# Both inverse transforms of a spectral block: frequencies 256 to 291, real and imaginary, in one chunk of 128 rows

## The chip, the cores and the metric

The kernel runs on one core of one Trainium2 chip. The metric is the time of one launch in device microseconds (us), the median of several runs. Lower is better.

## The reference

One adaLN block with two branches, forward and backward in one launch. `x` is 2048 x 576. A conditioning vector `c` gives six rows (`sa, ca, ga, sb, cb, gb`) by `silu(c) @ w_mod`. Cut to what matters:

```python
h = _layernorm(x) * (1 + ca) + sa
X = jnp.fft.rfft2(h)                      # 2048 x 289, complex
y = jnp.fft.irfft2(X * (w_r + 1j * w_i), s=(2048, 576))
x = x + ga * y
h = _layernorm(x) * (1 + cb) + sb
x = x + gb * (((h @ w_gate) * (h @ w_up)) @ w_down)     # 576 -> 4608 -> 576
```

The outputs are this `x` and the gradients (the vector-Jacobian product with `grad_out`) of `A_x`, `w_r`, `w_i`, `w_gate`, `w_up`, `w_down`, `c` and `w_mod`. The backward pass holds a second spectral chain of the same form, with the conjugate filter. So there are two inverse transforms: one in the forward pass, giving `y`, and one in the backward pass, giving the gradient of `h`.

## The kernel before

Everything is in bf16 with float32 sums in PSUM. The 2048 rows lie as 16 tiles of 128 (`NT = 16`). A transform over rows and columns is made of matmuls with tables: `RD` (real transform of the 576 columns), `G1` and `BD2` (the 2048 rows, split into 128 x 16), and for the way back `BDA`, `GB` and `IR`.

The order of the program is this. Tile pools lie in SBUF as two stacks, left and right, and a tile that takes over bytes of an earlier one waits until that one has been read. A scheduler orders the instructions of each engine when the program is built. Each engine and each DMA-issuing queue (SP, POOL) then works strictly in that order.

1. Forward, first stage (0 to 64 us): norm, columns, rows of the first transform (`s1_*`, zp and vp).
2. Forward, chunk stage (64 to 131 us): 19 chunks of up to 16 frequencies (`NCH = 19`). `s2_turn`, `s2_filter`, `s2_back`, `s2_inv` go through each. `s2_inv` (L420) ends with the first half of the inverse transform along the rows, in PSUM (`ap_`), and ScalarE copies it to `A_h`: 128 x 2 (real, imaginary) x 16 tiles x 292 frequencies (`FP = 292`, of which 289 are real ones).
3. Forward inverse transform, third stage (131 to 206 us), one step per tile `sa`. `s3_rows` (L449) ends the transform along the rows for three groups of 128 frequencies, starting at 0, 128 and 164 (`FS`; the last overlaps the second, and `IR` is zero for rows counted twice). Each group needs two matmuls of 256 columns, `upa` for two groups, `upb` for the third. ScalarE copies `upa` to `ut`, VectorE copies `upb` (L459). `s3_cols` (L461) goes back to 576 columns: for each half of 288 columns, six matmuls (three groups by real and imaginary) into `yp` (L471), so 12 per tile. `s3_norm` adds the residual and normalizes; it loads `xc` (L481) and turns the result by a DMA transpose into `h2T` (L499).
4. As a filler in stages 2 and 3 and alone until 300 us: `u4_group` (L351), the product of `grad_out` with `w_down`. It loads `wdn` (L358), turns it by DMA transpose into `wdT` (L359), multiplies into `u4p` (L364), stages into two buffers `ghh_st`, and POOL's queue writes these to `ghhT_d` (L367).
5. The middle (300 to 1262 us): the gated product and its gradients: gup (L611), u8p (L640) and the weight gradients u57p (L558). Weight gradients are copied to `so`, turned by DMA transpose into `woT` (L569) and stored. `product` of index 0 reads `gon`, the scaled `grad_out`, which lies at the top of a long-lived pool, up to byte 77536 of each partition.
6. Backward, first stage (1262 to 1364 us): `t1_*`, with the last u57p as filler. SP loads `n2c`, `goc`, `yc` (L813) for two tiles at a time. csA, csB, csC (L747) are sums over rows for the gradient of `c`. `trp` (L844) turns `gyr`, a ring of three buffers.
7. Backward, chunk stage (1364 to 1428 us): `t2_*`, again 19 chunks. `t2_inv` (L955) fills `A_`, the backward counterpart of `A_h`. `filter_grad` makes the gradients of `w_r` and `w_i` from `Xn`, loaded by POOL. The filler is now u3p (L1091), the down projection: 16 tiles x 2 halves x 36 matmuls. It needs `hl` (L1077), and `w_down` as `wdA` (blocks 0 to 14) and `wdB` (15 to 35), loaded by SP (L1066).
8. Backward inverse transform (1428 to 1480 us): `t3_rows` (L980), `t3_cols` (L992, yp at L1000), `t3_norm` (L1004, with csD, csE, and ScalarE's and VectorE's jk, u, ob). Here ScalarE copies both parts of `ut` (L989, L990). `opca_h` is a row that `t3_norm` needs; SP loads it (L709).
9. The rest of u3p, the remaining `filter_grad`s and the gradients of `c` and `w_mod` (to 1610 us).

`RD` and `IR` share one slot of SBUF (tag `tA`), once in each pass, and so do `G1` and `GB` (`tB`). POOL loads `IR` and `GB` in the backward pass.

Of the kernel before, what the change touches and what calls it, by code (L numbers as in the profile page):

```python
# [9 lines left out]
FP32 = mybir.dt.float32  # L10
BF = mybir.dt.bfloat16
# [3 lines left out]
ACT = mybir.ActivationFunctionType  # L15
# [4 lines left out]
NT = 16  # L20
S = 2048
D = 576
DP = 640
DF = 289
FP = 292
# [10 lines left out]
def _tables():  # L36
    f8 = np.float64
    q = np.arange(128)
    RD = np.zeros((128, 5, 2, FP), f8)
    f = np.arange(DF)  # L40
    for m in range(5):
        d = 128 * m + q
        valid = d < D
        ang = 2 * np.pi * np.outer(d, f) / D
        RD[:, m, 0, :DF] = np.cos(ang) * valid[:, None]
        RD[:, m, 1, :DF] = -np.sin(ang) * valid[:, None]
    t = np.arange(16); k1 = np.arange(128)
# [17 lines left out]
    for fc in range(3):  # L65
        ff = FS[fc] + q
        valid = (ff < DF) & (ff >= 128 * fc)
        cf = np.where((ff == 0) | (ff == DF - 1), 1.0, 2.0) / (D * S) * valid
        ang = 2 * np.pi * np.outer(ff, d) / D
        IR[:, fc, 0, :] = np.cos(ang) * cf[:, None]  # L70
        IR[:, fc, 1, :] = -np.sin(ang) * cf[:, None]
# [8 lines left out]
TABS = dict(RD=[128, 5, 2, FP], G1=[128, NT, 3, 128], GB=[128, NT, 3, 128], BD2=[128, 128], BDA=[128, 128], IR=[128, 3, 2, D])  # L80


def build(ctx, tc, A_x, A_w_r, A_w_i, B_w_gate, B_w_up, B_w_down, c_in, w_mod, grad_out,
          out_0, out_1, out_2, out_3, out_4, out_5, out_6, out_7, out_8):
    nc = tc.nc
# [57 lines left out]
    def norm_stats(xt, pool, nt, name, rstd_out, room=None):  # L143
# [43 lines left out]
    with ExitStack() as hs:  # L187
# [185 lines left out]

        u4_groups(4)
        r1.close()
        A_h = pool("hA", 1).tile([128, 2, NT, FP], BF, name="A_h")
        with ExitStack() as rc:
            c2 = pool("hc2", 2, "right", stack=rc)
            hwm = pool("hwm", 2, "right", stack=rc)
# [40 lines left out]
            def s2_inv(ci):  # L420
                g0, ng, f0, w = dims(ci)
                ap_ = fps.tile([128, 4, 128], FP32, name="ap_", tag="fp")
                for j in range(ng):
                    nc.tensor.matmul(ap_[:, j, :], lhsT=YTs[ci][:, j, :], rhs=T["BDA"][:], start=True, stop=True)
                Ac = A_h[:].rearrange("k c a f -> k (c a) f")[:, :, f0:f0 + w].rearrange("k e (j f) -> k j e f", f=4)
                evac(Ac, ap_[:, 0:ng, :].rearrange("k j (e f) -> k j e f", f=4), eng="a")

            def s2_fill(ci):
                u4_groups(2)
# [17 lines left out]
        uts, ybs, h2_made = {}, {}, []  # L447

        def s3_rows(sa):  # L449
            ut = uts[sa] = hw2.tile([128, 3, 256], BF, name="ut", bufs=3)  # L450
            upa = fps.tile([128, 2, 256], FP32, name="upa", tag="fp")
            upb = fps.tile([128, 2, 256], FP32, name="upb", tag="fp")
            for fc in range(3):
                f0 = FS[fc]
                o = upa[:, fc, :] if fc < 2 else upb[:, 0, :]
                nc.tensor.matmul(o, lhsT=A_h[:, 0, sa, f0:f0 + 128], rhs=T["GB"][:, sa, 1:3, :].rearrange("k v s -> k (v s)"), start=True, stop=False)
                nc.tensor.matmul(o, lhsT=A_h[:, 1, sa, f0:f0 + 128], rhs=T["GB"][:, sa, 0:2, :].rearrange("k v s -> k (v s)"), start=False, stop=True)
            evac(ut[:, 0:2, :], upa[:], eng="a")
            evac(ut[:, 2, :], upb[:, 0, :], eng="v")  # L459

        def s3_cols(sa):  # L461
            ut = uts[sa]
            if sa % 2 == 0:
                ybs[sa // 2] = hw2.tile([128, 2, D], BF, name="yb")
            yb = ybs[sa // 2]
            for h in range(2):
                yp = fps.tile([128, 512], FP32, name="yp", tag="fp")
                k = 0
                for fc in range(3):
                    for cc in range(2):  # L470
                        nc.tensor.matmul(yp[:, 0:288], lhsT=ut[:, fc, cc * 128:(cc + 1) * 128], rhs=T["IR"][:, fc, cc, h * 288:(h + 1) * 288], start=(k == 0), stop=(k == 5))  # L471
                        k += 1
                evac(yb[:, sa % 2, h * 288:(h + 1) * 288], yp[:, 0:288], eng="a")

        def s3_norm(sa):
# [211 lines left out]
    with ExitStack() as ts:  # L687
# [24 lines left out]
        T = {}  # L712
# [206 lines left out]
        with ExitStack() as r2:  # L919
# [35 lines left out]
            def t2_inv(ci):  # L955
                g0, ng, f0, w = dims(ci)
                ap_ = ps_fp.tile([128, 4, 128], FP32, name="apt", tag="fp")
                for j in range(ng):
                    nc.tensor.matmul(ap_[:, j, :], lhsT=YTs[ci][:, j, :], rhs=T["BDA"][:], start=True, stop=True)
                nc.scalar.copy(A_[:].rearrange("k c a f -> k (c a) f")[:, :, f0:f0 + w].rearrange("k e (j f) -> k j e f", f=4), ap_[:, 0:ng, :].rearrange("k j (e f) -> k j e f", f=4))  # L960

            def t2_grad(ci):
                if ci % 4 == 0:
# [14 lines left out]
        uts, ld3 = {}, {}  # L978

        def t3_rows(sa):  # L980
            ut = uts[sa] = c3.tile([128, 3, 256], BF, name="ut", bufs=3)
            upa = ps_fp.tile([128, 2, 256], FP32, name="upa", tag="fp")
            upb = ps_fp.tile([128, 2, 256], FP32, name="upb", tag="fp")
            for fc in range(3):
                f0 = FS[fc]
                o = upa[:, fc, :] if fc < 2 else upb[:, 0, :]
                nc.tensor.matmul(o, lhsT=A_[:, 0, sa, f0:f0 + 128], rhs=T["GB"][:, sa, 1:3, :].rearrange("k v s -> k (v s)"), start=True, stop=False)
                nc.tensor.matmul(o, lhsT=A_[:, 1, sa, f0:f0 + 128], rhs=T["GB"][:, sa, 0:2, :].rearrange("k v s -> k (v s)"), start=False, stop=True)
            nc.scalar.copy(ut[:, 0:2, :], upa[:])  # L989
            nc.scalar.copy(ut[:, 2, :], upb[:, 0, :])  # L990

        def t3_cols(sa):  # L992
            ut = uts[sa]
            gh = ghr3[:, sa % 3, :]
            for h in range(2):
                yp = ps_fp.tile([128, 512], FP32, name="yp", tag="fp")
                k = 0
                for fc in range(3):
                    for cc in range(2):
                        nc.tensor.matmul(yp[:, 0:288], lhsT=ut[:, fc, cc * 128:(cc + 1) * 128], rhs=T["IR"][:, fc, cc, h * 288:(h + 1) * 288], start=(k == 0), stop=(k == 5))  # L1000
                        k += 1
                nc.scalar.copy(gh[:, h * 288:(h + 1) * 288], yp[:, 0:288])

        def t3_norm(sa):  # L1004
# [186 lines left out]
```

## Time and profile before

| what | value |
|---|---|
| median of 3 runs | 1605.65 us (1599.14, 1605.65, 1614.77) |
| the profiled execution | 1611.72 us, span 1609.9 us |
| PE busy | 1542.1 us, 96% of the span |
| PE weight loads busy | 1041.0 us, 65% |
| VectorE (DVE) busy | 1038.4 us, 65% |
| ScalarE (ACT) busy | 559.1 us, 35% |
| GpSimd (POOL) busy | 170.4 us, 11% |
| yp, 192 matmuls in each transform | 1.47 us for 12 in the chain of waits |
| copy of upb to ut, 16 in each pass | 417 ns (VectorE, forward), 378 ns (ScalarE, backward) |

The span is from the first to the last instruction of the profiled execution; its time has some 2 us around that. Matmuls are pipelined, so a group's mean (286 ns for yp) is longer than the distance from one to the next. "L471" is line 471 of the kernel. In the chain of waits, each piece is what the next one waited for, followed back from the last instruction. DMA share is the mean busy share of the 16 DMA engines; packets that wait behind each other can bring it above 1.

### The profile page before, as it was taken

Reading aid. Unit: us, or ns where it says so; the run is one execution under the profiler, and the core shown is the slowest. Engines: PE = TensorE matmul, PEld = TensorE weight load, DVE = VectorE, ACT = ScalarE, POOL = GpSimd, SP = SyncE. Lnnn points to the kernel's source line nnn. Section 1 sums busy time; section 2 is a strip of 40 time slices with the busy share of each in tenths; the row PEclk is TensorE's granted clock in tenths of the full one; section 3 lists DMA queues with packets and bytes.
Section 4 is the critical chain, followed back from the end, with each engine's and each line's share of the span. In section 5 each row is a group of like instructions: output and inputs, shape, how many; then the busy total and the mean of one; then the engine's idle time right before and its main releaser. Section 6 shows DMA issues by size and latency. Waiting matters only on the chain.

```text
span 1609.9 us, 29989 instructions
## 1 busy us (share of the span) xinstructions
PE 1542.1 (96%) x11354; PEld 1041.0 (65%) x11354; DVE 1038.4 (65%) x2610; ACT 559.1 (35%) x1108; POOL 170.4 (11%) x284
## 2 busy tenths in 40 slices
PE   6999959999999999999999999999999979899997
PEld 4666624466766666666766666666667666677775
DVE  6765743566666666666666666666666765678656
ACT  6666712322222222222222222222222365466022
POOL 0001311100101010000101010100100011100232
PEclk9999979999999999999999999999999999999998
DMA  9978998488778677685767877776866786636775
GB/s 320 278 213 230 266 191 193 134 149 158 146 149 145 139 145 151 129 165 116 159 149 136 159 138 146 137 164 114 169 123 132 193 256 195 227 114 180 281 216 162
DMA packets 482995, 280.36 MB, mean 174 GB/s; under 512 B 405377, under 2 KB 450178, under 8 KB 481954
## 3 DMA queue, kind: packets, MB, share of 16 engines
q1 hardware_dynamic: 457666, 185.38, 55.4%
q0 software_dynamic: 25184, 93.07, 19.6%
q8 instruction: 88, 1.44, 0.4%
q14 instruction: 57, 0.47, 0.1%
HBM read 108.51 MB, written 82.31 MB: 119 GB/s over the span
## 4 chain that ended last, share of the span: by engine, by line
PE 77%; DMA 11%; DVE 5%; ACT 3%; issue 3%; POOL 0%; SPq 0%; DVEq 0%; ACTq 0%; POOLq 0%
PE u57p L558 25%; PE u8p L640 17%; PE gup L611 15%; PE u4p L364 7%; DMA ghhT_d<-ghh_st 2%; PE gup L606 2%; PE u3p L1091 2%; DMA Xn<-xn_d 2%; DMA n2c<-n_d 1%; DMA wdB<-in_B_w_down_dram 1%; DMA xc<-in_A_x_dram 1%; DMA x1t<-x_d 1%; PE yp L471 1%; PE zp L316 1%; PE yp L1000 1%
## 5 line engine op out<-in xcount | busy, mean ns | idle before, releaser
L645 DVE TENSOR_TENSOR acc<-acc,u8p 128x288 f32<-128x288 f32 x1088 | 488.6, 453 | 315.1 <-PE u8p L640 314.7
L640 PE MATMUL u8p<-wT,ggT 128*128 128x288 bf16 x1152 | 327.5, 286 | 1.2 <-DVE acc L645 1.2
L640 PE MATMUL u8p<-wT,guT 128*128 128x288 bf16 x1152 | 327.2, 286 | 0.0
L611 PE MATMUL gup<-h2T,wgu 128*128 128x512 bf16 x1152 | 295.4, 379 | 0.0
L561 ACT CAST so<-u57p 128x288 bf16<-128x288 f32 x216 | 86.0, 398 | 520.6 <-PE u57p L558 512.3
L558 PE MATMUL u57p<-gon,hh_sf 128*128 128x288 bf16 x1152 | 188.6, 286 | 0.2 <-DMA hh_sf<-hhT 0.2
L558 PE MATMUL u57p<-h2p,gg_sf 128*128 128x288 bf16 x1152 | 187.6, 286 | 0.0
L558 PE MATMUL u57p<-h2p,gu_sf 128*128 128x288 bf16 x1152 | 186.3, 286 | 0.0
L364 PE MATMUL u4p<-goT,wdT 128*128 128x512 bf16 x720 | 165.2, 384 | 18.6 <-ACT ghh_st L139 15.6
L611 PEld LDWEIGHTS <-wgu 128*128 128x128 bf16 x1152 | 109.5, 98 | 98.9 <-issue 17.5
L640 PEld LDWEIGHTS <-ggT 128*128 128x128 bf16 x1152 | 112.6, 98 | 67.2 <-issue 14.0
L640 PEld LDWEIGHTS <-guT 128*128 128x128 bf16 x1152 | 112.7, 98 | 55.3 <-issue 1.8
L1091 PEld LDWEIGHTS <-hl 128*128 128x128 bf16 x1152 | 111.7, 98 | 36.5 <-issue 8.5
L364 PEld LDWEIGHTS <-wdT 128*128 128x128 bf16 x720 | 70.2, 99 | 98.1 <-issue 23.6
L558 PEld LDWEIGHTS <-hh_sf 128*128 128x128 bf16 x1152 | 112.6, 98 | 28.8 <-DMA hh_sf<-hhT 0.5
L558 PEld LDWEIGHTS <-gu_sf 128*128 128x128 bf16 x1152 | 112.5, 98 | 28.4
L558 PEld LDWEIGHTS <-gg_sf 128*128 128x128 bf16 x1152 | 112.5, 98 | 28.3
L613 ACT CAST gT<-gup 128x512 bf16<-128x512 f32 x144 | 84.4, 586 | 129.7 <-PE gup L611 129.7
L613 ACT CAST uT<-gup 128x512 bf16<-128x512 f32 x144 | 84.3, 585 | 75.9 <-PE gup L611 73.0
L1091 PE MATMUL u3p<-wdB,hl 128*128 128x288 bf16 x672 | 95.3, 289 | 6.5 <-DMA wdB<-in_B_w_down_dram 5.6
L141 DVE CAST ghh_st<-u4p 128x512 bf16<-128x512 f32 x56 | 38.7, 690 | 75.0 <-PE u4p L364 55.4
L624 POOL DMA_DIRECT2D hhT_d<-hhT x36 | 33.2, 921 | 505.2 <-DVE hhT L615 476.2
(356 smaller groups left out, 1726.7 us busy)
## 6 DMA issues: line engine op xcount, KB each, us to landing
ghhT_d<-ghh_st POOLq DMA_DIRECT2D x36, 512.0 KB, 4.7
ghh<-ghhT_d POOLq DMA_DIRECT2D x36, 512.0 KB, 7.6
hhT_d<-hhT POOLq DMA_DIRECT2D x36, 512.0 KB, 6.7
hl<-hhT_d SPq DMA_DIRECT2D x32, 576.0 KB, 7.4
out_dram<-woT SPq DMA_DIRECT2D x72, 128.0 KB, 2.0
wdn<-in_B_w_down_dram SPq DMA_DIRECT2D x18, 288.0 KB, 3.6
out_dram<-so SPq DMA_DIRECT2D x36, 144.0 KB, 2.6
wgu<-in_B_w_up_dram POOLq DMA_DIRECT2D x18, 256.0 KB, 5.6
```

The lines of the kernel that those rows point to most:

```text
L141: nc.vector.tensor_copy(dst, src)
L316: mm = nc.tensor.matmul(zp[:, :FP], lhsT=hTs[t][:, m, :], rhs=T["RD"][:, m, cc, :], start=(m == 0), stop=(m == 4))
L364: nc.tensor.matmul(pt[:], lhsT=wdTs[k][:, j, m, :], rhs=goT[:, 4 * sb4:4 * sb4 + 4, m, :], start=(m == 0), stop=(m == 4))
L558: mm = nc.tensor.matmul(pw[0][:, 0:288], lhsT=sf[:, t, :], rhs=rhs_n[:, t, h * 288:(h + 1) * 288], start=(t == 0), stop=(t == NT - 1))
L561: nc.scalar.copy(so[:, h * 288:(h + 1) * 288], pw[0][:, 0:288])
L606: nc.tensor.matmul(pts[-1][:], lhsT=wgu[r, 8, jw * 128:(jw + 1) * 128], rhs=h2T[r, 4 * sb4:4 * sb4 + 4, 4, :], start=True, stop=False)
L611: nc.tensor.matmul(pts[k][:], lhsT=wgu[:, 4 * wi_ + m, jw * 128:(jw + 1) * 128], rhs=h2T[:, ts_, m, :], start=False, stop=(m == 3))
L613: nc.scalar.copy((gT, uT)[wi_][:, ts_, :], pts[k][:])
L624: nc.gpsimd.dma_start(hhT_d[:, :, fb, :].rearrange("tp f x -> f tp x"), hhT[:].rearrange("f (tp ti) p -> f tp (ti p)", ti=2))
L640: nc.tensor.matmul(pu[:, 0:288], lhsT=l_, rhs=r_, start=(k == 0), stop=(k == len(mms) - 1))
L645: nc.vector.tensor_tensor(out=dst, in0=dst, in1=pu[:, 0:288], op=ADD)
L1091: mm = nc.tensor.matmul(p2[:, 0:288], lhsT=hls[fb // 9][:, fb % 9, ti * 128:(ti + 1) * 128], rhs=(wdA[:, fb] if fb < 15 else wdB[:, fb - 1 ...
```

## The change

The third group of frequencies is no longer 128 wide with a large overlap. `A_h` and `A_` keep frequencies 0 to 255 only. Frequencies 256 to 291 go to an extra tile, `At`, with three planes of 64 columns for each tile of rows: minus imaginary, real, imaginary. Its columns 36 to 63 are set to zero. With two adjoining planes as the stationary operand, one pair of matmuls of 128 columns gives real parts in rows 0 to 63 and imaginary parts in rows 64 to 127. So the third group has 128 rows in all instead of 2 x 128, the way back to columns has five matmuls per half instead of six, and `ut` has 640 columns instead of 768. The frequencies are also cut differently among the chunks of `IR`, which is now 128 x 5 x 576 instead of 128 x 3 x 2 x 576. Chunks 16, 17 and 18 of the chunk stage are copied by three ScalarE instructions, one for each plane. The tile `hpp` moves from a long-lived pool to a pool of the first stage.

```diff
-FS = [0, 128, FP - 128]
+FM = 256
...
-    IR = np.zeros((128, 3, 2, D), f8)
+    IR = np.zeros((128, 5, 1, D), f8)
...
+    def planes(pool, name):
+        A = pool.tile([128, 2, NT, FM], BF, name=name)
+        At = pool.tile([128, NT, 3, 64], BF, name=name + "t")
+        nc.gpsimd.memset(At[:].rearrange("k a c f -> k (a c) f")[:, :, FP - FM:64], 0.0)
+        return A, At
+
+    def keep_planes(A, At, ps, ng, f0, w):
+        if f0 < FM:
+            nc.scalar.copy(A[:].rearrange("k c a f -> k (c a) f")[:, :, f0:f0 + w].rearrange("k e (j f) -> k j e f", f=4), ps[:, 0:ng, :].rearrange("k j (e f) -> k j e f", f=4))
+            return
+        src = ps[:, 0:ng, :].rearrange("k j (c a f) -> k c j a f", c=2, a=NT)
+        for pl, c in ((0, 1), (1, 0), (2, 1)):
+            dst = At[:, :, pl, f0 - FM:f0 - FM + w].rearrange("k a (j f) -> k j a f", f=4)
+            if pl == 0:
+                nc.scalar.activation(out=dst, in_=src[:, c], func=ACT.Copy, scale=-1.0)
+            else:
+                nc.scalar.copy(dst, src[:, c])
+
+    def rows_back(A, At, sa, ps_a, ps_b, GB):
+        for fc in range(2):
+            for c in range(2):
+                nc.tensor.matmul(ps_a[:, fc, :], lhsT=A[:, c, sa, 128 * fc:128 * fc + 128], rhs=GB[:, sa, 1 - c:3 - c, :].rearrange("k v s -> k (v s)"), start=(c == 0), stop=(c == 1))
+        for k in range(2):
+            nc.tensor.matmul(ps_b, lhsT=At[:, sa, 1 - k:3 - k, :].rearrange("k c f -> k (c f)"), rhs=GB[:, sa, 1 + k, :], start=(k == 0), stop=(k == 1))
+
+    def cols_back(ut, yp, IR, h):
+        for k in range(5):
+            nc.tensor.matmul(yp[:, 0:288], lhsT=ut[:, 128 * k:128 * k + 128], rhs=IR[:, k, 0, h * 288:(h + 1) * 288], start=(k == 0), stop=(k == 4))
...
         hw2 = pool("hc1", 2, "right", stack=r1)
+        hpp = hw2.tile([128, 3, DP], BF, name="hpp", bufs=1)
+        nc.gpsimd.memset(hpp[:, :, D:DP], 0.0)
...
-        hpp = hp1.tile([128, 3, DP], BF, name="hpp")
-        nc.gpsimd.memset(hpp[:, :, D:DP], 0.0)
...
-        A_h = pool("hA", 1).tile([128, 2, NT, FP], BF, name="A_h")
+        A_h = planes(pool("hA", 1), "A_h")
...
-            ut = uts[sa] = hw2.tile([128, 3, 256], BF, name="ut", bufs=3)
+            ut = uts[sa] = hw2.tile([128, 640], BF, name="ut", bufs=3)
...
-            evac(ut[:, 0:2, :], upa[:], eng="a")
-            evac(ut[:, 2, :], upb[:, 0, :], eng="v")
+            rows_back(*A_h, sa, upa, upb[:, 0:128], T["GB"])
+            evac(ut[:, 0:512], upa[:].rearrange("f c s -> f (c s)"), eng="a")
+            evac(ut[:, 512:640], upb[:, 0:128], eng="v")
...
-        A_ = pool("rb", 1, "right", stack=rB).tile([128, 2, NT, FP], BF, name="j_A")
+        A_ = planes(pool("rb", 1, "right", stack=rB), "j_A")
...
```

`s2_inv` and `t2_inv` call `keep_planes` in place of their one copy, `s3_cols` and `t3_cols` call `cols_back`, and `t3_rows` calls `rows_back` as `s3_rows` does.

More of the change, by code (lines that the diff above doesn't have):

```diff
@@ L62, in _tables @@
                 BDA[q0, c0] = cs_; BDA[q1, c0] = -sn_; BDA[q0, c1] = sn_; BDA[q1, c1] = cs_
-    IR = np.zeros((128, 3, 2, D), f8)
+    IR = np.zeros((128, 5, 1, D), f8)
     d = np.arange(D)
[L65 to L71, printed above, removed]
+    for pl in range(5):
+        for half in range(2):
+            cc = pl % 2 if pl < 4 else half
+            f0 = 128 * (pl // 2) + 64 * half if pl < 4 else FM
+            ff = f0 + np.arange(64)
+            valid = ff < DF
+            cf = np.where((ff == 0) | (ff == DF - 1), 1.0, 2.0) / (D * S) * valid
+            ang = 2 * np.pi * np.outer(ff, d) / D
+            IR[64 * half:64 * half + 64, pl, 0, :] = (np.cos(ang) if cc == 0 else -np.sin(ang)) * cf[:, None]
     import ml_dtypes
@@ L77, in _tables @@
     return dict(RD=c(RD), G1=c(G1), GB=c(GB), BD2=c(BD2), BDA=c(BDA), IR=c(IR))
[L80 removed]
+TABS = dict(RD=[128, 5, 2, FP], G1=[128, NT, 3, 128], GB=[128, NT, 3, 128], BD2=[128, 128], BDA=[128, 128], IR=[128, 5, 1, D])
 def build(ctx, tc, A_x, A_w_r, A_w_i, B_w_gate, B_w_up, B_w_down, c_in, w_mod, grad_out,
@@ L424, in s2_inv @@
                     nc.tensor.matmul(ap_[:, j, :], lhsT=YTs[ci][:, j, :], rhs=T["BDA"][:], start=True, stop=True)
-                Ac = A_h[:].rearrange("k c a f -> k (c a) f")[:, :, f0:f0 + w].rearrange("k e (j f) -> k j e f", f=4)
-                evac(Ac, ap_[:, 0:ng, :].rearrange("k j (e f) -> k j e f", f=4), eng="a")
+                keep_planes(*A_h, ap_, ng, f0, w)
             def s2_fill(ci):
@@ L449, in s3_rows @@
         def s3_rows(sa):
-            ut = uts[sa] = hw2.tile([128, 3, 256], BF, name="ut", bufs=3)
+            ut = uts[sa] = hw2.tile([128, 640], BF, name="ut", bufs=3)
             upa = fps.tile([128, 2, 256], FP32, name="upa", tag="fp")
[L452 to L457, printed above, removed]
-            evac(ut[:, 0:2, :], upa[:], eng="a")
-            evac(ut[:, 2, :], upb[:, 0, :], eng="v")
+            upb = fps.tile([128, 512], FP32, name="upb", tag="fp")
+            rows_back(*A_h, sa, upa, upb[:, 0:128], T["GB"])
+            evac(ut[:, 0:512], upa[:].rearrange("f c s -> f (c s)"), eng="a")
+            evac(ut[:, 512:640], upb[:, 0:128], eng="v")
         def s3_cols(sa):
@@ L467, in s3_cols @@
                 yp = fps.tile([128, 512], FP32, name="yp", tag="fp")
[L468 to L472, printed above, removed]
+                cols_back(ut, yp, T["IR"], h)
                 evac(yb[:, sa % 2, h * 288:(h + 1) * 288], yp[:, 0:288], eng="a")
@@ L959, in t2_inv @@
                     nc.tensor.matmul(ap_[:, j, :], lhsT=YTs[ci][:, j, :], rhs=T["BDA"][:], start=True, stop=True)
-                nc.scalar.copy(A_[:].rearrange("k c a f -> k (c a) f")[:, :, f0:f0 + w].rearrange("k e (j f) -> k j e f", f=4), ap_[:, 0:ng, :].rearrange("k j (e f) -> k j e f", f=4))
+                keep_planes(*A_, ap_, ng, f0, w)
             def t2_grad(ci):
@@ L980, in t3_rows @@
         def t3_rows(sa):
-            ut = uts[sa] = c3.tile([128, 3, 256], BF, name="ut", bufs=3)
+            ut = uts[sa] = c3.tile([128, 640], BF, name="ut", bufs=3)
             upa = ps_fp.tile([128, 2, 256], FP32, name="upa", tag="fp")
[L983 to L990, printed above, removed]
+            upb = ps_fp.tile([128, 512], FP32, name="upb", tag="fp")
+            rows_back(*A_, sa, upa, upb[:, 0:128], T["GB"])
+            nc.scalar.copy(ut[:, 0:512], upa[:].rearrange("f c s -> f (c s)"))
+            nc.scalar.copy(ut[:, 512:640], upb[:, 0:128])
         def t3_cols(sa):
@@ L996, in t3_cols @@
                 yp = ps_fp.tile([128, 512], FP32, name="yp", tag="fp")
[L997 to L1001, printed above, removed]
+                cols_back(ut, yp, T["IR"], h)
                 nc.scalar.copy(gh[:, h * 288:(h + 1) * 288], yp[:, 0:288])
```

## The prediction

> **What bounds the kernel now.** I read the windows by stage first, to see where TensorE (PE) is full and where it is not; then the chain of waits in the two stages that the change touches; then the issue queue of the loads around the second one.
>
> Windows by stage; columns are start:end, length, busy time (and instructions) of PE, PEld, DVE, ACT, POOL, granted clock, DMA share, GB/s. The lines are: the chunk stage that feeds the first inverse transform, that transform with its filler (four lines), the 920 us middle, the gap ahead of the last part, the backward chunk stage, and the backward inverse transform.
>
> ```profile
> 80.00:130.00 50.00, 50.00 (x414) 30.84 (x414) 34.28 (x98) 34.31 (x67) 4.78 (x9) 1.00 0.72 204
> 130.00:152.00 22.00, 21.80 (x145) 13.58 (x144) 12.31 (x37) 14.24 (x30) 3.79 (x7) 1.00 1.07 241
> 152.00:175.00 23.00, 22.06 (x146) 13.82 (x144) 16.43 (x51) 16.88 (x34) 5.40 (x10) 1.00 1.00 269
> 175.00:207.00 32.00, 30.28 (x191) 18.44 (x189) 21.44 (x66) 20.27 (x41) 9.96 (x18) 1.00 1.10 251
> 207.00:230.00 23.00, 8.31 (x28) 3.15 (x28) 8.10 (x23) 3.98 (x7) 3.25 (x6) 0.66 1.20 146
> ...
> 330.00:1250.00 920.00, 920.00 (x6623) 623.78 (x6622) 604.99 (x1457) 233.80 (x463) 66.75 (x95) 1.00 0.75 144
> ...
> 1365.00:1380.00 15.00, 8.60 (x86) 6.11 (x85) 6.58 (x19) 4.79 (x9) 1.84 (x4) 0.95 1.05 394
> 1380.00:1428.00 48.00, 47.03 (x464) 34.24 (x464) 36.25 (x110) 26.92 (x56) 4.94 (x9) 0.95 0.40 134
> 1428.00:1480.00 52.00, 49.78 (x433) 37.97 (x432) 41.45 (x106) 35.89 (x78) 1.61 (x3) 1.00 0.58 172
> ```
>
> PE is nearly full in both transforms (130 to 200 and 1428 to 1480). But during the first one the DMA share is 1.00 or more throughout, and behind it PE stands still for 14.7 of 23 us; during the second one the DMA engines are at 0.58 and PE stays full behind it.
>
> The chain of waits in the first transform: PE until 175, transfers after.
>
> ```profile
> 171.64 2.16 PE u4p L364 x10
> 173.80 1.48 PE yp L471 x12
> ...
> 178.54 4.90 DMA xc<-in_A_x_dram
> ...
> 185.79 5.85 DMA xc<-in_A_x_dram
> ...
> 208.33 19.82 DMA ghhT_d<-ghh_st
> ```
>
> In the second transform, one turn of two tiles, 6.80 us from one yp to the next:
>
> ```profile
> 1441.09 1.60 PE yp L1000 x12
> 1442.77 0.33 ACT ghr L1002
> 1443.14 0.88 ACT u L1019
> ...
> 1444.78 0.76 DVE jk L1015 x2
> ...
> 1447.01 0.29 ACT ghr L1002
> 1447.89 1.60 PE yp L1000 x12
> ```
>
> PE between 1365 and 1380, in order of time; the bracket is the idle time and its releaser. The down-projection's filler (u3p) waits for its weights.
>
> ```profile
> 1367.57 0.41 PE L1091 MATMUL u3p<-wdB,hl 128*128 128x288 bf16 x2 [1.30 <-DMA wdB<-in_B_w_down_dram]
> ...
> 1370.74 0.79 PE L1091 MATMUL u3p<-wdB,hl 128*128 128x288 bf16 x5 [0.85 <-DMA hl<-hhT_d]
> ...
> 1380.15 1.12 PE L1091 MATMUL u3p<-wdB,hl 128*128 128x288 bf16 x4 [4.33 <-DMA wdB<-in_B_w_down_dram]
> ```
>
> **The change, part by part.** The matmuls' true pace is in the chain: 12 yp take 1.47 us, 122.5 ns each; one 256-column upa or upb takes 0.11 us; four 128-column xp, each with weights of its own, take 0.22 us, 55 ns each. (The 286 ns of the groups are pipelined.)
>
> (a) Matmuls. Per tile, two of 12 column matmuls go: 2 x 0.1225 = 0.245 us. Of six row matmuls two shrink from 256 to 128 columns: 2 x (0.11 - 0.055) = 0.11 us. That is 0.355 us a tile, 5.7 us for 16 tiles, 11.4 us in both transforms. The Trainium skill ("TensorE: Matmul & The Clock Gate", Back-to-back issue gap) speaks against the small ones: a stream of weight loads and matmuls is said to hold about 81 ns at 128 columns. By that rule the shrunken pair saves 2 x 29 ns, and the two transforms together lose 1.7 us of the gain; the trace's xp at 55 ns differs.
>
> (b) The backward transform. If PE set its pace, all 5.7 us would come. But the turn above runs through ScalarE and VectorE: yp 1.60, ghr, u, jk, ob, u, ghr, then ut and yp again. There only the yp on the turn shrinks, by 0.25: 8 turns x 0.25 = 2.0 us. The built order puts two more u3p matmuls into each turn, 8 x 2 x 0.1225 = 2.0 us of later work done early. So 4.0 to 5.7 us; behind it PE is 99.6% busy (49.8 of 50 us from 1480), so what is saved reaches the end. I take 4.5, nearer the turn.
>
> (c) The forward transform. Bounds 0 and 5.7. Speaking for the low end: the DMA share is at 1.00 from 130 to 262, the SP queue between 60 and 262 stands 46.6 us in 11 waits of the wdn load (L358) for the wdT transposes, and the xc loads stand behind those. The 14.7 us hole at 207 to 230 ends when a ghhT_d write lands, and both staging buffers (ghh_st) are full by then, so a PE that arrives sooner waits longer. Speaking for the high end: until 175 the chain is PE, for ten tiles (3.55 us). I take half of these, 1.8.
>
> (d) Smaller copies. VectorE's and, in the backward stage, ScalarE's second copy of ut falls from 256 to 128 columns (418 and 378 ns now); neither is on the turn. Chunks 16 to 18 get three ScalarE copies instead of one: 3 x 0.38 (the 128x256 row) for 0.59, so +0.55 each for two, and two more of 0.30 to 0.38 for the last: +1.8 us of ScalarE per stage. ScalarE is busy 34.3 of 50 and 26.9 of 48 us there, the row matmuls of upa need only chunks 0 to 15, and PE has u4p or u3p to do. I take 0; with the cover gone upb would wait some 0.75 us in each transform, 1.5.
>
> (e) Two new memsets on POOL of 128x1344. Nearest row: 128x512 in 0.52 us, so 0.5 to 1.4 us. The first is ahead of the first ghhT_d write (issued at 70), over buffers of the first stage, which are free by 60; the second is ahead of the load of T_GB (issued 1365, needed 1427) and of Xn. I take 0; bare, 1.4. hpp only changes its place. The IR table shrinks from 864 to 720 KB, twice, far ahead of its use: 0.
>
> (f) Addresses, and so the order of loads. IR was the larger tenant of its slot (6912 bytes per partition, RD has 5840). With 5760 the slot follows RD, and in the last stage everything above moves down by 1056 bytes. wdA now begins below the end of gon, which the weight-gradient matmuls (u57p) still read. In the built order both wdA loads move on SP from among the n2c loads (1294 and 1299) to behind the so store (1334 now), around the last two woT transposes (1346, 1354). Also opca_h's place now overlaps the gyr ring, so its load waits for the last transposes (trp) of gyr on PE, at 1361, and it stands ahead of the hl and wdB loads. Before, the first hl left at 1354.
>
> What is won: 2160 KB leave the time from 1294 to 1308, where PE waited 7.1 us in three waits (csA for n2c). Two of them, and a short one for gxr, 0.23 + 0.30 + 1.77, are inside wdA's flight; the third (5.05, at 1316 to 1321) is inside wn's (2336 KB, 10.4 us). Bounds 0 and 7.1; I take 2.3.
>
> What is lost: from 1361 SP has 2 x 576 + 1440 + 576 + 1584 = 4752 KB to fetch until the last wdB is in, and POOL 720 + 1536 KB: 7008 KB, 7.2 MB, at the 403 GB/s of these us (394 to 413) 17.8 us, until 1379; now it is 1380.15. So the late start costs little: the first loads had been ahead of a queue that was full anyway. Also the built order has 30 wdA and then 20 wdB matmuls ready before the last wdB, with three chunk steps, as many as now. Bounds -1 (1379 against 1380) and +9.5 (6.9 us of late start, and 1008 KB at 400 GB/s, 2.6). I take +1, near the calculation.
>
> Sum: -4.5 - 1.8 - 2.3 + 1.0 = -7.6 us. The profiled execution took 1611.7 us (span 1609.9), so it would take 1604.1; it lies 6.1 us above the median of 1605.65, so I forecast 1598 for the median, 0.5% less. By the Trainium skill's figure for narrow matmuls (its page and section above) it would be some 0.8 us more (half of 1.7, since half of the saved time counts).
>
> **Rivals.**
> 1. The queue decides, slower. Place: SP at opca_h. If the hl and wdB loads are bound by their start and not by the bytes, the hole at 1365 to 1380 grows by 9.5 us, and the half-speed clock behind a hole lasts longer (0.50 in 1380 to 1385 now). The gains must be at their low end, 4.0 + 0 + 0: +5.5, 1611. It decides once the last wdB lands more than about 8 us later than now relative to the end of u57p (1354 to 1380, 26 us). For it: hl now lands while the queue has room (0.95 at 1355 to 1360). Against: 394 to 413 GB/s from 1365 to 1380.
> 2. All of it comes. The forward transform gives its 5.7 us since its chain up to 175 is PE, the backward one 5.7, and the n2c waits go whole, 7.1: -18.5 plus 1 for the queue, -17.5, 1588. For it: PE at 97 to 99% in both. Against: the DMA share, and wn's own flight.
> 3. Only the matmuls of the backward turn count, the moved loads cancel: -4, 1602. It differs from the forecast by less than single runs do.
>
> **How the numbers follow.** A measurement of this kernel tells about 1% from no change (16 us; three runs spread from 1599 to 1615). Forecast 0.45, with rival 3 0.10 beside it; rival 1 0.20; rival 2 0.25. Faster by over 1% means below 1589.6: rival 2 for the most part, and the lower tail of the forecast: 0.30. Slower by over 1% means above 1621.7: rival 1 with the covers of (d) and (e) gone as well (5.5 + 1.5 + 1.4) and a high median: 0.14. Within 1%: 0.56. The range reaches from rival 2 less 5 us of spread, 1583, to rival 1 with spread, 1615.
>
> **What would show it.** (a) 160 yp matmuls per transform at 122 ns, upb at about 55 ns. (b) Turns of 6.4 to 6.6 us in the backward transform, and PE still full behind it. (c) A hole of PE behind the forward transform at the same time as now, as long or longer. (f) wdA leaving after the so store; fewer n2c waits of csA; the first hl leaving about 7 us after the last u57p, and the last wdB landing about 25 us after it. I am wrong if the middle of 920 us changes its length, if the hole at 207 shrinks by more than 4 us, or if the hole ahead of the backward chunks changes by more than 5.

## The result, and the profile after

The changed kernel takes 1598.68 us (median of 20 runs, 1592.37 to 1609.65), the kernel before 1606.8 us in the same session (20 runs, 1599.14 to 1617.66). The ratio is 0.9949, 95% interval 0.9928 to 0.9970: 8.1 us less, between 4.8 and 11.6. The forecast was 7.6 us less, 1598.0. The profiled execution has a span of 1602.5 us against 1609.9.

Windows by stage of the changed kernel, with the columns of the table shown for before (start:end, length, busy time of PE, PEld, DVE, ACT, POOL, granted clock, DMA share, GB/s). Behind 1250 us the windows are moved by 6 us, because the stages begin 6 us earlier.

```profile
130.00:152.00 22.00, 21.20 (x142) 12.95 (x141) 12.05 (x40) 16.06 (x36) 4.32 (x8) 1.00 1.11 246
152.00:175.00 23.00, 20.89 (x129) 12.65 (x128) 13.98 (x46) 15.96 (x34) 4.87 (x9) 0.93 1.10 248
175.00:207.00 32.00, 26.71 (x159) 15.27 (x157) 20.90 (x67) 19.43 (x40) 9.23 (x17) 0.95 1.04 253
207.00:230.00 23.00, 15.45 (x58) 6.13 (x57) 11.69 (x31) 4.41 (x9) 4.17 (x8) 0.78 1.11 260
330.00:1250.00 920.00, 920.00 (x6622) 623.97 (x6620) 604.11 (x1454) 234.91 (x465) 66.75 (x95) 1.00 0.75 143
1359.00:1374.00 15.00, 9.85 (x80) 6.62 (x80) 8.62 (x24) 5.34 (x11) 4.73 (x11) 0.89 1.02 385
1374.00:1422.00 48.00, 43.97 (x448) 32.39 (x447) 36.31 (x109) 27.59 (x61) 4.57 (x9) 0.96 0.51 171
1422.00:1474.00 52.00, 49.56 (x445) 37.57 (x445) 42.63 (x111) 35.24 (x81) 0.37 (x1) 1.00 0.55 162
```

Three things are to be seen. During the forward transform (130 to 207) PE is now idle for 8.2 of 77 us, where it was idle for 2.9. The hole behind it (207 to 230) has 7.55 us of idle time instead of 14.7. The chunk stage of the backward part (1374 to 1422) has 4.0 us of idle time where it had 1.0.

The idle time in the forward transform is a wait for ut. PE's timeline of the changed kernel, the bracket being the idle time and what ended it:

```profile
159.92 1.62 PE L186 MATMUL yp<-T_IR,ut 128*128 128x288 bf16 x6 [2.11 <-DVE ut L143]
...
179.58 0.91 PE L186 MATMUL yp<-T_IR,ut 128*128 128x288 bf16 x6 [2.11 <-DVE ut L143]
...
222.59 7.22 PE L395 MATMUL u4p<-goT,wdT 128*128 128x512 bf16 x20 [7.25 <-ACT ghh_st L141]
```

VectorE's timeline ahead of the first of these tells why ut is late. The addition of xc stands in front of the copy of ut on the same engine, and it waits for the load of xc:

```profile
157.78 0.46 DVE L509 TENSOR_TENSOR x<-x,xc 128x576 bf16<-128x576 bf16 x1 [4.12 <-DMA xc<-in_A_x_dram]
...
159.58 0.28 DVE L143 CAST ut<-upb 128x128 bf16<-128x128 f32 x1
```

The backward turn, from the chain of waits (start, duration, what):

```profile
1450.52 0.80 PE yp L186 x5
...
1451.34 0.09 ACT ghr L1016
...
1451.64 0.87 ACT u L1033
...
1452.79 0.50 ACT ut L1007
...
1454.40 0.69 DVE jk L1029 x2
...
1456.31 0.48 ACT ut L1007
...
1456.84 0.80 PE yp L186 x5
```

Two tiles take 6.32 us where they took 6.80. Only one half of a tile's yp (five matmuls, 0.80 us) lies on the turn now; before, both halves did (x12, 1.60 us). In their place ScalarE's copies of upa to ut (L1007) now lie on it.

SP's queue at the end of the preceding stage, and what PE does next (SP's timeline, then PE's):

```profile
1345.47 0.58 SPq L1080 DMA_DIRECT2D wdA<-in_B_w_down_dram  x1
...
1350.80 0.58 SPq L1080 DMA_DIRECT2D wdA<-in_B_w_down_dram  x1
...
1356.15 0.35 SPq L731 DMA_DIRECT2D opca_h<-modb_d  x1
1356.54 1.12 SPq L1091 DMA_DIRECT2D hl<-hhT_d  x2
```

```profile
1362.69 1.65 PE L1105 MATMUL u3p<-wdA,hl 128*128 128x288 bf16 x6
...
1374.52 1.12 PE L1105 MATMUL u3p<-wdB,hl 128*128 128x288 bf16 x6 [4.49 <-DMA wdB<-in_B_w_down_dram]
```

wdA leaves behind the weight gradients, opca_h stands ahead of hl, and the first u3p runs at 1362.7. By the first backward yp 228 u3p matmuls are done; before, 262.

Read from these two executions alone, the forward part has gained 6.2 us (first gup at 291.8 instead of 298.0), the backward transform 5.6 us (from its first yp to the end of its last, with the u3p between them taken off), and the late loads have cost 4.2 us (34 u3p fewer, at 0.1225 us each). This was theory A of the first four experiments (there with 6.1 and 4.4), against the prediction's own terms. Both were too trusting of one pair of profiles, as the experiments show.

### The profile page after: what moved, and what is told of

It is laid out like the page before. It is cut to its first block, busy times and chain, and to the rows that moved or that the text cites. A ratio compares the mean times of both kernels' runs of the same rounds, so it can differ in the third digit from the quotient of the medians.

```text
span 1602.5 us, 29892 instructions
## 1 busy us (share of the span) xinstructions
PE 1534.4 (96%) x11290; PEld 1034.2 (65%) x11290; DVE 1037.3 (65%) x2610; ACT 558.6 (35%) x1120; POOL 172.6 (11%) x286
## 4 chain that ended last, share of the span: by engine, by line
PE 78%; issue 7%; DMA 6%; DVE 4%; ACT 3%; POOL 1%; SPq 0%; POOLq 0%; ACTq 0%; DVEq 0%
PE u57p L580 25%; PE u8p L662 17%; PE gup L633 16%; PE u4p L395 7%; PE u3p L1105 4%; PE gup L628 2%; DMA Xn<-xn_d 2%; DMA n2c<-n_d 1%; PE zp L347 1%; PE zp L886 1%; ACT u L1033 1%; DMA n_d<-n 1%; DMA ghhT_d<-ghh_st 1%; DMA hh_sf<-hhT 0%; PE yp L186 0%
## 5 line engine op out<-in xcount | busy, mean ns | idle before, releaser
L662 PEld LDWEIGHTS <-ggT 128*128 128x128 bf16 x1152 | 112.6, 98 | 67.2 <-issue 14.0
L580 PEld LDWEIGHTS <-hh_sf 128*128 128x128 bf16 x1152 | 112.6, 98 | 29.2 <-DMA hh_sf<-hhT 0.9
L580 PEld LDWEIGHTS <-gu_sf 128*128 128x128 bf16 x1152 | 112.5, 98 | 28.5
L580 PEld LDWEIGHTS <-gg_sf 128*128 128x128 bf16 x1152 | 112.5, 98 | 28.2
L395 PEld LDWEIGHTS <-wdT 128*128 128x128 bf16 x720 | 70.1, 99 | 87.9 <-issue 14.8
```

Of the source, the lines that this page charges most:

```text
L395: nc.tensor.matmul(pt[:], lhsT=wdTs[k][:, j, m, :], rhs=goT[:, 4 * sb4:4 * sb4 + 4, m, :], start=(m == 0), stop=(m == 4))
L580: mm = nc.tensor.matmul(pw[0][:, 0:288], lhsT=sf[:, t, :], rhs=rhs_n[:, t, h * 288:(h + 1) * 288], start=(t == 0), stop=(t == NT - 1))
L662: nc.tensor.matmul(pu[:, 0:288], lhsT=l_, rhs=r_, start=(k == 0), stop=(k == len(mms) - 1))
```

## Experiments

All ratios are to the kernel before, on the same chip. A first group takes the change apart.

**One transform alone.** e1_fwd changes the forward transform only, e2_bwd the backward one only. Each keeps the old planes, rows and columns for the other, with a second table for it:

```
+    IRo = the old 3 x 2 table                     (both kernels)
 e1: T["IR"] = load_table(tl0, "IRo", "tA", nc.gpsimd)   # backward as before
 e2: T["IR"] = load_table(hp1, "IRo", "tA")              # forward as before
```

> Only the forward inverse transform is changed; the backward one keeps its 12 column matmuls, its planes and its 6912-byte table slot, so wdA and opca_h are loaded as before. Theory A, read from the two traces (the change gains 6.1 us ahead of the middle, 5.6 us in the backward transform, and loses about 4.4 us ahead of the backward chunks): the first gup comes some 6 us earlier than the 298.6 us of before, everything behind it is as before, and the time falls by 6 us, ratio 0.996. Theory B, the terms of the prediction (forward 1.8, backward 4.5, moved loads 1.3 won): the time falls by 1.8 us, ratio 0.999, and the first gup comes at about 297.

> Only the backward inverse transform is changed; the forward one and its memory are as before, while the last stage's table slot is the smaller one, so wdA and opca_h are loaded late as in the changed kernel. Theory A: first gup at 298.6 us as before; the backward transform (first yp to last yp) is shortened and has 18 more u3p matmuls in it, 5.6 us together; by the first backward yp some 34 u3p matmuls fewer are done than before (262), which gives 4.4 us back; net -1.2 us, ratio 0.999. Theory B (the terms of the prediction): -4.5 - 2.3 + 1.0 = -5.8 us, ratio 0.996, with about 254 u3p matmuls done by the first backward yp.

e1_fwd: 1601.74 us, ratio 0.9978 (0.9953 to 1.0002), first gup at 282.4. e2_bwd: 1598.23 us, ratio 0.9953 (0.9928 to 0.9977), first gup at 285.1. The interval of e1_fwd holds both theories. That of e2_bwd leaves out theory A's 0.999 and holds theory B's 0.996, but B had counted on 254 u3p by the first backward yp, and there were 228, as A had said. Neither theory has the first gup where it came: e2_bwd's instructions are, in the same order on every engine, those of before up to the last stage, and still its first gup came 13 us earlier than in the profile of before. PE's wait for ghh_st, the long one of 13.81 us in before, is this in e2_bwd:

```profile
215.99 19.11 PE L405 MATMUL u4p<-goT,wdT 128*128 128x512 bf16 x80 [2.78 <-ACT ghh_st L151]
```

So either a further table in DRAM matters, or this wait changes from one execution to the next.

**Late wdA or late opca_h.** e3_pad widens the last stage's table slot again; e4_opca gives opca_h a place of its own.

```
 e3: T[k] = load_table(tl0, k, tag, room=3456 if k == "RD" else 0)
     T["IR"] = load_table(tl0, "IR", "tA", nc.gpsimd, room=3456)
 e4: -opca_h = modh(MCA, "opca_h", c3b)
     +opca_h = modh(MCA, "opca_h", tl)
```

> The changed kernel, with the last stage's table slot widened back to 6912 bytes and nothing else edited. wdA then lies behind gon again, and both of its loads stand among the n2c loads on SP, as before; opca_h still shares the place of gyr, but now stands behind the first wdB load. Theory A (the late wdA costs the u3p filler ahead of the backward chunks): some 30 u3p matmuls more by the first backward yp than the 228 of the changed kernel, and about 4 us off its time, ratio to before 0.992 to 0.993. Theory B (the moved load wins 1.3 us net, as predicted): 1.3 us slower than the changed kernel, ratio 0.996, with longer waits for n2c. Theory C (the wait of opca_h in front of hl and wdB is what costs, not wdA): most of the 4 us too, because here opca_h stands further back; e4_opca tells it from A.

> The changed kernel, with opca_h in a place of its own (left side, 1152 bytes) in place of one that gyr held, so that its load on SP waits for nothing; wdA is still late. Theory A (the late wdA decides): no change against the changed kernel, ratio to before 0.995, u3p by the first backward yp still about 228. Theory C (opca_h's wait decides): hl and wdB leave up to 5.7 us earlier, up to 30 u3p matmuls more by the first backward yp, ratio 0.992 to 0.993.

e3_pad: 1597.84 us, ratio 0.9932 (0.9901 to 0.9964), 263 u3p done by the first backward yp. e4_opca: 1600.81 us, ratio 0.9962 (0.9936 to 0.9987), 227 u3p. By the count of u3p it is wdA and not opca_h, and e4_opca's interval leaves out the 0.992 to 0.993 that opca_h would have given. That the early wdA makes the kernel faster is not shown by the totals: e3_pad's interval holds 0.9949 as well. In e3_pad PE fills the waits of t1's last tiles with u3p, as before did and the changed kernel does not:

```profile
1352.74 0.29 PE L1105 MATMUL u3p<-wdA,hl 128*128 128x288 bf16 x1
...
1353.34 0.41 PE L1105 MATMUL u3p<-wdA,hl 128*128 128x288 bf16 x2
...
1359.04 0.78 PE L1105 MATMUL u3p<-wdA,hl 128*128 128x288 bf16 x5
```

Eighteen u3p run there before the first chunk's matmul (xp); with a late wdA there are none.

**The same kernel again.** c1_same is the kernel of before, unedited; c2_twin reads the backward table from a second, equal copy in DRAM.

```
 c2: T["IR"] = load_table(tl0, "IRo", "tA", nc.gpsimd)   # IRo equal to IR
```

> The kernel of before once more, instruction for instruction. In e2_bwd the forward part has exactly the instructions and the order of before, and yet its first gup came at 285.1 us where before has 298.05, and the PE idle time that ghh_st ends at some 210 to 230 us was 2.8 us where before has 13.8. Theory N (the length of that hole changes from one execution to the next, with the landing of the ghhT_d write): this second profile of the same kernel shows another hole, anywhere from 2 to 14 us, a first gup between 285 and 300, and from the first gup to the end 1312 us to within 2; ratio 1.000 within 0.3%. Theory P (the hole belongs to the kernel of before): hole 13 to 15 us and first gup at 297 to 299 again.

> The kernel of before with one edit: the backward transform loads its table from a second copy of the same table in DRAM, as e1_fwd and e2_bwd did; same instructions, same order, same results. Theory N (execution to execution): ratio 1.000 within 0.3%. Theory M (a further table in DRAM moves what lies where and so speeds up the forward part, which would explain why e2_bwd was 0.5% faster although its forward part was that of before): ratio 0.995 and a first gup at 285 to 287.

c1_same: 1606.01 us, ratio 1.0010 (0.9980 to 1.0040), first gup at 302.7. c2_twin: 1604.97 us, ratio 0.9998 (0.9973 to 1.0024), first gup at 288.3. So a second table shows no effect, and the first gup of one and the same forward program came at 285.1, 288.3, 298.1 and 302.7 us in four executions, the last a little outside the 285 to 300 that theory N expected. PE's waits in c1_same, where before had one of 2.58 and one of 13.81:

```profile
209.50 7.07 PE L364 MATMUL u4p<-goT,wdT 128*128 128x512 bf16 x25 [3.73 <-DVE ghh_st L141]
225.38 6.49 PE L364 MATMUL u4p<-goT,wdT 128*128 128x512 bf16 x20 [8.80 <-ACT ghh_st L139]
```

The 6.2 us that the forward part seemed to gain lie well inside this. The expected 1312 us from the first gup to the end was missed too: it was 1317.8 in c1_same and 1317.4 in c2_twin.

**PE time of the forward transform put back; both repairs together.**

```
 e6: +nc.tensor.matmul(yp[:, 0:288], lhsT=ut[:, 0:128], rhs=more, start=True, stop=False)   # more: zeros
      upb: rhs=GB[:, sa, k:2 + k, :], 256 columns, the last 128 copied
 e5: the slot at 6384 bytes (room=3192), opca_h in tl
```

> The changed kernel with TensorE's work of the forward transform put back: a sixth column matmul per half, against a table of zeros, and upb 256 columns wide; planes, copies, addresses and the backward transform stay changed. It also has POOL's order of before (the ghh load ahead of the y_d store). Theory A (the forward transform's PE time sets the pace: its 5.7 us come back): 5.7 us slower than the changed kernel, ratio to before 0.9985. Theory N (behind the forward part PE waits for ghhT_d in any case, so PE time there is worth little): as the changed kernel within 2 us, ratio 0.995; yp matmuls 192 in the forward part.

> The changed kernel with the last stage's table slot at 6384 bytes, just enough for wdA to lie behind gon and to be loaded early, and with opca_h in a place of its own. From the stage times so far (from the first gup to the end: 1312 us before, 1310.2 to 1312.3 with the late wdA, 1307.0 in e3_pad): 1306 to 1307 us from the first gup to the end and some 262 u3p matmuls by the first backward yp; about 4 us less than the changed kernel, ratio to before 0.992. Rival (early wdA helped e3_pad only by chance): no better than the changed kernel, ratio 0.995, and 1310 or more behind the first gup.

e6_fpe: 1600.54 us, ratio 0.9968 (0.9936 to 1.0000), against 0.9949 for the changed kernel: 3 us between them, within the intervals, so that neither theory is excluded. e5_both: 1599.38 us, ratio 0.9956 (0.9924 to 0.9988), 263 u3p by the first backward yp, but 1309.2 us from the first gup to the end, where 1306 to 1307 were expected, and a first gup as late as 298.7. The rival's 0.995 lies in the interval and the expected 0.992 just outside it; the time behind the first gup lies between the two views (the rival had 1310 or more). So e5_both does not show the gain that was expected of an early wdA.

**Four staging buffers.** The forward part's spread hides what its shorter transform is worth, so the last group takes away the largest wait in it, the one for ghh_st.

```
-sts[fb] = u4w.tile([128, NT, 128], BF, name="ghh_st", bufs=2)
+sts[fb] = (u4w if not u4r or fb % 4 < 2 else u4r[0]).tile([128, NT, 128], BF, name="ghh_st", bufs=2)
```

g1_bef4 has it on the kernel of before, g2_aft4 on the changed kernel, g3_pad4 on e3_pad, g4_fpe4 on e6_fpe.

> The kernel of before with four staging buffers for ghh_st behind the chunk stage in place of two; PE, DVE and ACT keep their instructions and order. In the executions so far PE stood 2.8 to 13.8 us at 207 to 240 us for a ghh_st buffer whose ghhT_d write had not landed, and the first gup came between 285 and 303 us. Theory H (the two buffers pass the lateness of that write on to PE): the wait of u4p for ghh_st at 207 to 240 goes below 1 us, the first gup comes at 280 to 286, the time falls by some 8 us, ratio 0.995. Theory D (the DMA engines' work decides, share 1.0 and more from 130 to 230 us): PE waits as long for something else behind it (wdT, or the first wgu), the first gup stays at 285 to 303, ratio 1.000.

> The changed kernel with the same four staging buffers. Under theory H this shows what the shorter forward transform is worth once its lateness is no longer swallowed by the wait for ghhT_d: first gup some 5 us before that of g1_bef4, ratio to before 0.988 to 0.990. Under theory D, or if the forward transform is not what PE is late by, first gup as in g1_bef4 to within 2 us and a ratio of 0.995.

> The changed kernel with four staging buffers and with the 6912-byte table slot in the last stage (wdA early), the candidate for the fastest. Early wdA has been worth 2.7 us from the first gup to the end so far (1308.1 us mean of two executions against 1310.9 of four). Under theory H: ratio to before 0.987, 1307 to 1309 us behind the first gup; under theory D: 0.993.

> g2_aft4 with TensorE's work of the forward transform put back (a sixth column matmul per half against zeros, upb 256 columns wide), as in e6_fpe. If PE time there counts once the buffers are four: first gup 5 to 6 us later than in g2_aft4 and 0.35% slower than it. If PE waits for data in any case: the same to within 2 us.

g1_bef4: 1597.48 us, ratio 0.9953 (0.9923 to 0.9983). g2_aft4: 1589.34 us, 0.9917 (0.9888 to 0.9945). g3_pad4: 1587.17 us, 0.9912 (0.9876 to 0.9949). g4_fpe4: 1588.62 us, 0.9912 (0.9876 to 0.9947). Theory H holds: the hole is gone from all four. The window of g1_bef4 behind the transform, where before had 8.31 us of PE and a clock of 0.66:

```profile
207.00:230.00 23.00, 23.00 (x108) 10.37 (x107) 13.36 (x28) 6.03 (x11) 4.93 (x10) 1.00 1.13 268
```

The DMA share there is 1.13, as high as with the hole (1.20 in before, 1.11 in the changed kernel); what the buffers changed is whether PE feels it. In g1_bef4 the order of the loads on SP and POOL changed as well (both wgu loads of POOL moved behind later ghhT_d writes). In g2_aft4 POOL's order is exactly that of the changed kernel, ghhT_d writes issued from 200 to 240 us took up to 11.0 us to land, and PE waited for no ghh_st; so it is the buffers and not POOL's order. (On SP the loads of the rows ga_h and opcb_h stand later in both kernels; that was not tried alone.) The first gup comes at 276.1 (g1, even ahead of the 280 to 286 expected), 283.4 (g2), 274.1 (g3) and 276.9 (g4). The expectations that g2_aft4's first gup would be 5 us ahead of g1_bef4's, and that g4_fpe4's would be 5 to 6 us behind g2_aft4's, both failed, and the totals of g2_aft4 and g4_fpe4 do not differ: the PE time put back into the forward transform costs nothing that shows. g3_pad4's 0.987 was missed too, though its 1303.8 us behind the first gup are less than the 1307 to 1309 expected. g2_aft4 has one wait of 6.16 us for ut at 198.7 that the other three do not have.

## The fourteen executions side by side

Times in us. "ut" and "ghh_st": PE's idle times of 0.5 us and more ahead of yp and of u4p behind 130 us (g2's 1.9 is a wait for wdT). "forward": from the start of the first yp of the forward transform to the end of its last; in all fourteen 151 u4p run meanwhile. "t1 and chunks": from the first zp of the last stage to the first backward yp; "backward": from there to the start of the last tile's yp; both less 0.1225 us for each u3p done meanwhile.

| kernel | forward PE work | first gup | ut | forward | ghh_st | wdA | t1 and chunks | backward | first gup to end |
|---|---|---|---|---|---|---|---|---|---|
| before | old | 298.1 | 0.9 | 67.5 | 18.2 | early | 108.3 | 45.3 | 1311.9 |
| c1_same | old | 302.7 | 1.6 | 68.4 | 19.8 | early | 111.5 | 45.3 | 1317.8 |
| c2_twin | old | 288.3 | 3.2 | 69.9 | 7.9 | early | 112.5 | 45.3 | 1317.4 |
| g1_bef4 | old | 276.1 | 0.9 | 67.5 | 0 | early | 110.9 | 45.3 | 1315.8 |
| e1_fwd | new | 282.4 | 5.1 | 67.4 | 5.4 | early | 110.3 | 45.9 | 1312.0 |
| e2_bwd | old | 285.1 | 3.9 | 70.6 | 4.1 | late | 113.7 | 40.0 | 1310.2 |
| after | new | 291.8 | 8.2 | 72.8 | 7.3 | late | 112.6 | 39.9 | 1310.7 |
| e4_opca | new | 286.9 | 3.9 | 65.0 | 11.5 | late | 114.5 | 39.7 | 1312.3 |
| e6_fpe | old | 288.9 | 3.1 | 70.2 | 8.6 | late | 112.3 | 39.9 | 1310.2 |
| g2_aft4 | new | 283.4 | 8.9 | 72.7 | 1.9 | late | 113.1 | 40.0 | 1308.7 |
| g4_fpe4 | old | 276.9 | 1.9 | 68.7 | 0 | late | 113.3 | 40.0 | 1307.9 |
| e3_pad | new | 292.2 | 6.9 | 70.1 | 10.8 | early | 110.1 | 42.1 | 1307.0 |
| e5_both | new | 298.7 | 6.7 | 68.3 | 16.9 | early | 112.6 | 40.3 | 1309.2 |
| g3_pad4 | new | 274.1 | 3.8 | 66.3 | 0 | early | 108.1 | 41.2 | 1303.8 |

## Why the prediction was right, step by step

**The total.** 1598.7 against 1598.0, and within 1%. That the two lie so near each other is luck: the backward transform was argued rightly from the trace and gave a little more than forecast, but the term of the forward transform cannot be found in the runs, the term of the addresses has the wrong sign, and some 2.3 us lie at a place that has no term.

**(a) The matmuls: right.** There are 160 yp in each transform. PE's timeline of the changed kernel in the backward transform gives the pace from start to start:

```profile
1445.44 0.60 PE L180 MATMUL upa<-T_GB,j_A 128*128 128x256 bf16 x4
1445.88 0.28 PE L182 MATMUL upb<-T_GB,j_At 128*128 128x128 bf16 x2
1445.99 0.29 PE L762 MATMUL csE<-ghr,pick 128*128 128x288 bf16 x1
```

Four upa take 0.44 us, two upb 0.11: 110 and 55 ns each. The Trainium skill ("TensorE: Matmul & The Clock Gate", Back-to-back issue gap) has about 81 ns for a matmul of 128 columns in a stream of weight loads and matmuls; this trace does not agree, and its 55 ns decide.

**(b) The backward transform: right, slightly small.** Predicted 4.5 of 5.7. The column "backward" falls from a mean of 45.4 (five kernels, 45.3 to 45.9) to 39.9 (six with the late wdA, 39.7 to 40.0): 5.5 us. In the three with the early wdA it is 40.3 to 42.1; what makes them longer was not looked into. The step that was too small is the turn: the prediction took 0.25 us from it and forecast turns of 6.4 to 6.6 us, but it lost 0.48. One half of the yp left the turn altogether, 0.80 us, and on balance 0.32 came back in other pieces, among them ScalarE's two copies to ut of 0.50 and 0.48 us.

**(c) The forward transform: forecast at 1.8 us, and on the mean nothing is left.** Predicted 1.8 of 5.7, because the queues behind it would swallow the rest. It is swallowed earlier. The seven executions with the old PE work wait 2.2 us for ut on the mean (0.9 to 3.9), the seven with the new one 6.2 (3.8 to 8.9): of 5.7 us of PE time, 4.0 come back as waits for ut. VectorE's copy of ut, which stands behind the addition of xc, ended 61% of this waiting in the seven new ones; ScalarE's copy ended the rest. After some of these waits PE also runs slower. In the changed kernel the granted clock was 0.50 from 160 to 162 us and 0.60 from 180 to 182, behind the two waits shown above; the six yp at 159.92 take 1.62 us, the six at 179.58 still 0.91. Over the whole transform the clock is 1.00 in all seven old executions but 0.95 in two of the new ones and 0.97 to 0.98 in two more. By an estimate (the missing share of the clock times the length) this is another 1.5 us on the mean of the seven.

The column "forward" shows the outcome: 67.5 to 70.6 us in the seven old executions and 65.0 to 72.8 in the seven new ones, with a mean of 69.0 and of 68.9. The new ones spread too widely to tell 0 from 1.8, but no pair of runs shows a gain clear of its interval either: with the old PE work e6_fpe is 3.0 us slower than the changed kernel and g4_fpe4 0.8 us faster than g2_aft4. (In both pairs two loads on POOL and one on SP stand in another place as well.) The prediction named the late xc loads, but in (d) it kept VectorE's copy of ut out of the reckoning as not on the turn; in the forward transform PE waits for it. That sentence was wrong.

The prediction's own condition, that it would be wrong if the hole at 207 us shrank by more than 4 us, came true (13.8 to 7.3 us for its longest wait). It was a bad condition: the same forward program shows 2.8, 6.6, 8.8 and 13.8 us in four executions. Its other two conditions did not come true: from the first gup to the last u8p it is 986.0 us before and 986.1 after, and PE is idle for 5.2 us of the 15 ahead of the backward chunks where it was for 6.4.

**(d), (e).** The memset of the backward planes took 1.23 us on POOL (1360.7), inside the 0.5 to 1.4 that were estimated; no wait of PE for it was found. The extra copies of chunks 16 to 18 cost nothing that shows in the backward part: with an early wdA "t1 and chunks" has a mean of 110.7 in the five executions with the old planes and of 110.3 in the three with the new ones.

**(f) The last stage's addresses: wrong in both halves.** Predicted: 2.3 us won at the n2c waits, 1.0 lost. Nothing was won: PE's waits for n2c sum to 6.7 to 9.5 us in the eight executions with an early wdA (mean 8.2) and to 7.2 to 8.4 in the six with a late one (mean 8.0). And more was lost: "t1 and chunks" rises from a mean of 110.5 to 113.2, 2.7 us. So the term is +2.7 where -1.3 stood, 4.0 us off. The step that failed is "the late start costs little". It held that as many u3p would be ready with a late wdA; but 18 of them had filled waits of t1 before the chunk stage began, and these are lost.

Its count of bytes failed too. It divided them by the 403 GB/s of 1365 to 1375, but over 1361 to 1380 the kernel before moved 372, and from 1356, when opca_h leaves, to 1380.5 the changed kernel moved 355. The last wdB landed 24.3 us after opca_h had left and not 17.8; by an estimate the lower rate explains 2.4 of these 6.5 us (7.2 MB at 355 GB/s are 20.2 us), and the rest was not followed up. Measured from the end of the last u57p, it landed after 30.3 to 31.4 us in the six executions with a late wdA and after 26.0 to 27.9 in the eight with an early one; some 25 had been forecast. In e4_opca the first hl left 4.1 us after the last u57p, where it left after 7.5 in the changed kernel, and the last wdB still took 30.8. How the 2.7 us divide between the lost u3p and the later wdB was not tried.

**The sum.** With -5.5 for (b), 0 for (c) and +2.7 for (f) it would be -2.8, outside the measured interval. More lies behind the backward transform: from the start of the last tile's yp to the end, less 0.1225 us for each u3p left, it is 24.7 to 30.0 us in the five kernels with the old backward transform (mean 27.9) and 24.5 to 27.1 in the six with the new one and a late wdA (mean 25.6). These 2.3 us bring the sum to -5.1, inside the interval of -4.8 to -11.6 and 3 us short of its middle. Some 0.25 of them are the two matmuls less in the last tile; what causes the rest was not tried and stays open, and since e1_fwd, with the old transform, is at 24.7 it may be in part the spread between executions. With it the stage times agree with the other runs within their intervals: 0 for e1_fwd (measured -3.5, from -7.5 to +0.3), -5.1 for e2_bwd and for e6_fpe (measured -7.5, from -11.6 to -3.7, and -5.1), -5.1 between g1_bef4 and g2_aft4 (-5.8) or g4_fpe4 (-6.6).

**The rivals.** Rival 1 had the right sign at its place (the late loads do cost) but the wrong one of the two loads: opca_h's wait on SP, freed in e4_opca, changed nothing that shows. Relative to the last u57p the last wdB landed 5.3 us later than before, short of the 8 from which it was to decide. Rival 2 failed at the forward transform and at n2c. Rival 3 was right that the forward transform gives nothing; it failed at the turn, and the moved loads do not cancel.

The kernel with the lowest median here is g3_pad4, 1587.17 us, 0.9912 (0.9876 to 0.9949) of before: the change, wdA early again, and four staging buffers. Its lead over g4_fpe4 (0.9912 as well) and g2_aft4 (0.9917) is not shown by the totals. It has the shortest time behind the first gup, 1303.8 us, but its profiled execution was also the fastest of its eight.

## What to carry to other kernels

Profile the unchanged kernel a second time before explaining a difference of a few microseconds between two profiles: here the forward part moved by 17.6 us between executions of the same instructions, while the unchanged backward transform stayed within 0.6 us over five, and only such a stage can be compared singly. When matmuls are taken out of a stage that is 96% full (74.1 of 77 us here), look for the next operand that PE would wait for and what stands in front of its producer on that engine. A table that gets smaller moves every address above it: look up which loads then overlap a tile still in use, and which filler matmuls those loads had fed.

## What the runs showed of the hardware that was not expected

With the DMA share at 1.0 and more (1.02 to 1.20 from 207 to 230 us), the landing of a 512 KB write is not a stable number: the ghhT_d writes have a median of 4.3 us over the whole changed kernel, and between 190 and 240 us they took up to 19.8 us in before, 17.4 in c1_same, 8.3 in e2_bwd and 8.5 in g1_bef4. Two more staging buffers take this spread off PE: they cut some 8 us from the kernel of before (0.9953, from 0.9923 to 0.9983), about as much as the whole change does.
